# Seven experts in the order of their row counts, with tails of 64, 32 and 0 rows, and a new table of the attention's order

## The chip, the cores and the metric

The kernel runs on one core of one Trainium2 chip. The metric is the device time of one execution in microseconds. Before the change it is 722.44 us, the median of three runs (721.05 to 723.35).

## The reference

An RWKV-7 attention over 4 batches, 8 heads, 768 steps and a head width of 40 gives 3072 tokens of 320 numbers. Each token then goes through one of eight experts, whose sizes are set by the data:

```python
state_decay = state * w_t - outer(state @ a_t, b_t)      # per head, step by step
state = state_decay + outer(v_t, k_t)                    # y_t = r_t @ state, taken before the update
...
logits = x @ w_gate                                      # x: 3072 x 320, 8 experts
expert = argmax(logits);  gate = softmax(logits)[expert]
y[rows of e] = relu(x[rows of e] @ w1[e]) @ w2[e]        # w1: 320 x 1024, w2: 1024 x 320
out = gate * y
```

No row is dropped, so a kernel with fixed block sizes needs a way for the rows that do not fit.

## The kernel before, in words

**Attention.** The 768 steps are cut into 12 chunks of 64, and a chunk is done for two batches at a time: 24 units (`unit(u)`, from L574 on). A unit is some 19 groups of small matmuls on PE (TensorE), with copies, masks, scans and decays between them on ACT, DVE and POOL (ScalarE, VectorE, GpSimd). Names used below: `scan_r`, `scan_q` are scans on DVE; `decay_kb`, `decay_a`, `s2`, `gt_mask`, `st` and `tt_add` (L749) are elementwise work on POOL; `p_last` is the last group of the inverse, `kept` its three copies out of PSUM (two for one half, one for the other), `tt_add` adds to what they left, and `p_q` (operands `TT,O`) is the group that reads it; `t_v` transposes V, `t_u` and `t_st` transpose U and the state, `p_x` (operand `turn_gate`) turns the result and computes the logits.

**The order.** All of this, and the routing and expert 0 with it, is written as `Step` objects with an engine, a cost in us and what they read and write. `in_order` simulates the engines with those costs and issues the steps in the order of that simulation. For units 2 to 22 the order on PE, ACT, DVE and POOL is taken from the table `CYCLE`: for each named step an engine and a key, and `unit + key` is its rank. For steps on SP (loads and stores, SyncE's queue) the key is only a tie-break. PE executes in the order in which it was issued: where the simulated data come earlier than the real ones, PE waits.

**Routing.** After units, `route` works on the logits of one or two chunks: it picks each token's expert (`choose`), counts tokens ahead of it with matmuls, turns the count into a slot (`place`, L1010 to 1035) and adds the token's number to a table `tab` at that slot by a matmul of one-hot rows and columns. Five passes run on POOL, the last two on DVE. The table has 28 columns of 128 slots: for each pair of experts three columns of the first, three of the second, and a column with 64 tail rows of each. `rows_at` turns table entries into gather and scatter indices with 12 small DVE operations. After the last but one pass the counts are raised to at least 384 (L1015), and `g_idx` and `s_idx` are computed for all main columns; after the last pass only the four tail columns are (`gh_idx`, `sh_idx`). So every expert's first 384 rows are known before the last chunk is, and a tail holds the rest, up to 448 rows in all (`CAP`).

**Expert 0** is part of the planned block: its three gathers from `x_rows`, the three of expert 1 and the tail of both share two buffers (`qini`, L1112), each gathered block is turned by three transposes (L1122), and expert 0's 384 rows go through layer 1 and layer 2. Expert 1's weights are loaded into room that the attention frees (`wx`), by SP, while the last units run.

**Experts 1 to 7** follow in a loop (L1274 on). Layer 1 (`layer1`, from L1207 on) multiplies by 448 columns of rows: for each pair of 128 hidden units four whole matmuls (L1217) and two half-height ones (L1225). Every fp32 matmul appears as two in the records. Layer 2 (`layer2`, from L1235 on) has three blocks of 128 rows, each 8 matmuls of 320 columns; after the second expert of a pair comes a block with the tails of both, 64 and 64 rows, at the two halves of the array. Each block is copied by ACT (L1247) and scattered by POOL (L252). In the meantime the next expert's blocks are turned (`turn`, L1203), the next pair's seven blocks gathered (L1195), and the next expert's weights, 2.62 MB in eight transfers, fetched on ACT's queue (L240 to L246). Three rooms for weights are used in turn.

**Overflow.** Rows past 448 are gathered in blocks of 128 by a loop at the end under `tc.If(nx > 0)`; the number of these blocks, `nx`, is counted from the expert counts (L1169 to 1187).

The lines on which the experts' times hang (layer 1 from L1214, its half-height part L1222, and layer 2 from L1238):

```python
for db in range(DB - 1):                                    # L1217: whole matmuls, c1 - c0 columns of rows
    nc.tensor.matmul(hps[i][:, : c1 - c0], lhsT=w[0][:, db, (fb + i) * 128 : (fb + i + 1) * 128], rhs=xT[:, db, c0:c1], ...)
...
hf = slice(i * 64, (i + 1) * 64)                            # L1225: the last 64 of 320, at one half of the array's rows
nc.tensor.matmul(hps[i][:, : c1 - c0], lhsT=w[1][hf, fb // 2, :], rhs=xT[hf, DB - 1, c0:c1], ...)
...
for fb in range(FB):
    r0 = 0
    for w, h, c0, n in parts:                               # L1241: n rows of one expert; a pair's tails are two parts
        nc.tensor.matmul(zp[r0 : r0 + n], lhsT=h[:, fb, c0 : c0 + n], rhs=w[2][:, fb, :], ...)
        r0 += n
```

## Time and profile before

| | |
|---|---|
| median of three runs | 722.44 us |
| profiled execution, its own time | 722.41 us |
| its span | 720.7 us |
| mean granted TensorE clock | 0.98 |
| TensorE matmul busy | 657.8 us, 91% |
| GpSimd, VectorE, ScalarE busy | 402.6, 395.0, 281.4 us |
| DMA | 60.85 MB, mean 84 GB/s |

The profile is one execution. "PE" is matmuls, "PEld" weight loads, a name with a small q (SPq, ACTq) an engine's DMA queue. A line number is that of the kernel; many of the attention's matmuls share the helper L563, so they are told apart by operands. In a row of the timeline the first number is the start, the second the time from the first start to the last end of a run of like instructions, and the bracket is the idle time before it with what ended it. Matmuls are pipelined: the distance from start to start is what one costs in a row of many, not its own duration.

### The profile page before, as it was taken

The page shows a single profiled execution, that of the slowest core. Times are in us where ns is not written, and L with a number is a line of the kernel's source. Part 1 is how long each engine was busy: PE and PEld are TensorE (multiplying, and loading weights), DVE is VectorE, ACT ScalarE, POOL GpSimd, SP SyncE. Part 2 cuts the span into 40 slices and gives each one's busy share as a digit, 9 for nine tenths or more (in the row PEclk, how much of TensorE's full clock was granted, in tenths as well). Part 3 has the DMA queues.
Part 4 walks back from the last instruction along what each step waited for, and adds up shares of the span by engine and source line. Part 5 has one row for each costly group of instructions (what it writes and reads, how often), then busy time and mean ns, then how long its engine had stood idle before and what let it go on. Part 6 is the DMA issues. An engine that isn't in the chain of part 4 may idle for free.

```text
span 720.7 us, 32168 instructions
## 1 busy us (share of the span) xinstructions
PE 657.8 (91%) x13992; PEld 507.0 (70%) x13992; DVE 395.0 (55%) x864; ACT 281.4 (39%) x734; POOL 402.6 (56%) x599
## 2 busy tenths in 40 slices
PE   3679999989989999999889986999999999999995
PEld 2578889878888888889788875556655656464653
DVE  6578988878888988788887785302020101111010
ACT  3356656646556656566556642211011111101110
POOL 8877768897889789778986753132214014110101
PEclk9689999999999999999999999999999999999998
DMA  4432323233333323233322033228343244012000
GB/s 94 98 70 63 85 70 73 70 95 101 73 75 82 82 71 87 71 92 77 86 59 62 25 100 116 67 95 264 119 169 97 82 159 157 25 32 74 25 10 20
DMA packets 120355, 60.85 MB, mean 84 GB/s; under 512 B 100688, under 2 KB 116051, under 8 KB 120212
## 3 DMA queue, kind: packets, MB, share of 16 engines
q1 hardware_dynamic: 103176, 33.09, 18.6%
q10 hardware_dynamic: 13900, 16.23, 7.1%
q0 software_dynamic: 3136, 9.44, 4.0%
q8 instruction: 111, 1.82, 1.1%
q14 instruction: 32, 0.26, 0.1%
HBM read 50.08 MB, written 9.31 MB: 82 GB/s over the span
## 4 chain that ended last, share of the span: by engine, by line
PE 48%; issue 34%; POOL 9%; DMA 4%; DVE 2%; SPq 2%; ACT 1%; POOLq 0%; DVEq 0%; ACTq 0%
PE ps L563 39%; PE ps L667 6%; POOL out_dram L252 4%; PE ps L780 3%; POOL xg L1195 3%; SPq L598 2%; DMA qini<-x_rows,g_idx 1%; DMA KB<-in_packed_dram 1%; POOL KB L627 1%; DMA R<-in_packed_dram 1%; POOL TT L749 1%; DMA Vu<-in_packed_dram 0%; DMA out_dram<-q,s_idx 0%; DMA dec<-in_packed_dram 0%; DVE wx L690 0%
## 5 line engine op out<-in xcount | busy, mean ns | idle before, releaser
L1230 DVE TENSOR_SCALAR h_sb<-hp 128x448 f32<-128x448 f32 (+1 forms) x32 | 18.4, 575 | 191.0 <-PE hp L1225 164.6
L563 PE MATMUL ps<-wx 64*64 64x128 f32 (+1 forms) x3072 | 104.4, 267 | 7.3 <-issue 2.5
L690 DVE TENSOR_TENSOR wx<-ps,wx 64x256 f32<-64x256 f32 (+1 forms) x216 | 90.1, 417 | 26.3 <-PE ps L563 22.2
L677 POOL TENSOR_TENSOR wx<-T,ihalf 64x256 f32<-64x256 f32 x96 | 70.6, 736 | 47.7 <-DVE T L673 34.2
L252 POOL DMA_INDIRECT out_dram<-zo,s_idx x21 | 20.8, 992 | 134.8 <-ACT zo L1247 133.6
L563 PEld LDWEIGHTS ps<-wx 64*64 64x64 f32 x3072 | 81.8, 136 | 20.0 <-issue 11.2
L627 POOL TENSOR_TENSOR KB<-KB,rv 128x512 f32<-128x512 f32 x48 | 71.5, 1493 | 3.0 <-DMA R<-in_packed_dram 1.7
L1241 PE MATMUL zp<-w,h_sb 128*128 128x320 f32 (+1 forms) x272 | 71.0, 433 | 0.0
L1241 PEld LDWEIGHTS zp<-w,h_sb 128*128 128x128 f32 (+1 forms) x272 | 44.4, 174 | 20.5 <-issue 1.3
L723 DVE STREAM_TRANSPOSE wx<-ps 128x512 f32<-128x512 f32 x72 | 51.0, 708 | 12.3 <-PE ps L563 10.4
L552 ACT COPY wx<-ps 128x256 f32<-128x256 f32 (+2 forms) x102 | 43.9, 430 | 33.5 <-PE ps L563 25.9
L1231 ACT ACTIVATE h_sb<-hp 128x448 f32<-128x448 f32 (+1 forms) x32 | 16.1, 505 | 101.0 <-PE hp L1225 50.8
L1241 PE MATMUL zp<-wx,h_sb 128*128 128x320 f32 (+1 forms) x192 | 53.0, 433 | 0.0
L1247 ACT COPY zo<-zp 128x320 f32<-128x320 f32 x25 | 10.7, 427 | 106.0 <-PE zp L1241 96.0
L1217 PE MATMUL hp<-xgT,w 128*128 128x448 f32 x128 | 51.1, 547 | 0.0
L749 POOL TENSOR_TENSOR TT<-TT,wx 128x512 f32<-128x512 f32 x24 | 44.1, 1837 | 11.3 <-DVE pm__173 L965 5.8
L552 ACT COPY ZU<-ps 64x320 f32<-64x320 f32 x92 | 38.7, 421 | 14.4 <-PE ps L667 12.9
L615 DVE TENSOR_TENSOR_SCAN rv<-dec,ones 128x521 f32<-128x521 f32 x24 | 39.3, 1637 | 7.6 <-DMA dec<-in_packed_dram 6.0
L1241 PEld LDWEIGHTS zp<-wx,h_sb 128*128 128x128 f32 (+1 forms) x192 | 33.4, 177 | 13.2 <-issue 0.8
L1217 PEld LDWEIGHTS hp<-xgT,w 128*128 128x128 f32 x128 | 23.5, 190 | 25.8 <-issue 25.5
L667 PE MATMUL ps<-ident,Vu 128*128 128x128 f32 x184 | 30.0, 287 | 11.6 <-DVE rv L615 7.7
L563 PE MATMUL ps<-ZU,nKB 128*64 128x104 f32 (+1 forms) x768 | 39.0, 253 | 1.4 <-issue 1.0
(243 smaller groups left out, 1378.1 us busy)
## 6 DMA issues: line engine op xcount, KB each, us to landing
KB<-in_packed_dram SPq DMA_DIRECT2D x188, 40.0 KB
w<-in_moe_w_dram ACTq DMA_DIRECT2D x16, 320.0 KB
x_rows<-xs SPq DMA_DIRECT2D x24, 192.0 KB
w<-in_moe_w_dram ACTq DMA_DIRECT2D x8, 512.0 KB
dec<-in_packed_dram SPq DMA_DIRECT2D x96, 40.0 KB
Vu<-in_packed_dram SPq DMA_DIRECT2D x96, 40.0 KB
A<-in_packed_dram SPq DMA_DIRECT2D x92, 40.0 KB
R<-in_packed_dram SPq DMA_DIRECT2D x92, 40.0 KB
```

The costliest lines, as they stand in the source:

```text
L252: ins_ = nc.gpsimd.indirect_dma_start(out=out[:, :], out_offset=bass.IndirectOffsetOnAxis(ap=si, axis=0), in_=zo, in_offset=None, bounds_c ...
L552: nc.scalar.copy(dst, src)
L563: nc.tensor.matmul(out_, lhsT=lhsT, rhs=rhs, start=start, stop=stop, skip_group_check=True)
L615: Step(turn_of("scan_r", pre + 0.1), DVE, 1.5, lambda e: nc.vector.tensor_tensor_scan(rv[:, : SEG * C1 + 1][:, ::-1], dec[:, ::-1], ones65 ...
L627: Step(turn_of("decay_kb", pre), POOL, 1.24, lambda e, kb=kb, by=by: nc.gpsimd.tensor_tensor(kb, kb, by, op=ALU.mult), reads=hrv + hKB[2:] ...
L667: nc.tensor.transpose(psum[:, ps.at, p * 128 : (p + 1) * 128], t[:, p].rearrange("x a j -> x (a j)"), ident[:])
L677: Step(turn_of("s2", rk + 0.5), POOL, 0.85, lambda e, z=z, par=par, q=q, X=X: nc.gpsimd.tensor_tensor(X[halves[par], q, :, 2, :], T1[halve ...
L690: nc.vector.tensor_tensor(dst[o_, q], src[o_, q], old[o, q], op=ALU.add)
L723: Step(turn_of(f"x0{k}", rk - 0.4), DVE, 0.72, lambda e, ps=ps, Xn=Xn: nc.vector.transpose(Xn[:, :, :, 0, :], half_sums(ps, 2)[:, :, :, 0, ...
L749: Step(turn_of("tt_add", rk - 1.5), POOL, 1.45, lambda e, X=X, TT=TT: nc.gpsimd.tensor_tensor(TT[:], TT[:], X[:, :, :, 2, :], op=ALU.add), ...
L1217: nc.tensor.matmul(hps[i][:, : c1 - c0], lhsT=w[0][:, db, (fb + i) * 128 : (fb + i + 1) * 128], rhs=xT[:, db, c0:c1], start=(db == 0 and n ...
L1241: nc.tensor.matmul(zp[r0 : r0 + n], lhsT=h[:, fb, c0 : c0 + n], rhs=w[2][:, fb, :], start=(fb == 0), stop=(fb == FB - 1), skip_group_check ...
```

## The change

Expert 0 stays as it was, with a tail of 64 rows. The other seven are no longer run as 1 to 7 but by place: on the chip they are sorted by their final counts, the largest at place 1. The tail of a place is fixed: 64 rows at places 0 and 1, 32 at places 2 to 5, none at 6 and 7. A place's layer 1 has 384 columns and its tail; a pair's tail block has twice the tail rows, and the pair of places 6 and 7 has no tail block, gather or transpose of one. The table has four columns for each expert, 32 in all. Expert 0's three columns are turned into indices after the last but one pass. For the seven others the table is permuted by place and turned into indices after the last pass, so place 1's gathers and weights come after that too. Weights of places are fetched by SP, at an address that SP reads from the sorted list into a register. Behind the block a few small DVE operations work out each expert's cap for the overflow count.

The table `CYCLE` is new as a whole, and eight costs of steps are other numbers: `scan_r` 1.66 for 1.5, `scan_q` 1.45 for 1.6, `decay_kb` 1.57 for 1.24, `decay_a` 1.36 for 1.24, `tt_add` 1.95 for 1.45, `st` 0.8 for 0.85, `x0` 0.73 for 0.72 and `xs_pad` 0.3 for 0.2. In the order of units 2 to 22 that it gives, `kept` is on ACT with all three copies (one was on DVE), both `x14` copies on ACT (one was on DVE), one of the two `nkb` copies on DVE, `tt_add` follows `gt_mask` on POOL with a `decay_kb` behind it (which stood between them before), `t_st` and `t_u` change places on PE, and `t_v` runs one unit earlier, ahead of `p_x`.

The diff, cut to its core:

```diff
+    PJ = NJ + 1
+    TAIL = (64, 64, 32, 32, 32, 32, 0, 0)
-    NS = E // 2 * PB
+    NS = E * PJ
...
+    def by_count():
+        v = nc.vector
+        v.scalar_tensor_tensor(key[:], in0=ptr[:, 1:], scalar=16.0, in1=iota_f[:, : E - 1], op0=ALU.mult, op1=ALU.subtract)
+        v.tensor_tensor(
+            over[:], key[:, None, :].to_broadcast([128, E - 1, E - 1]), key[:].unsqueeze(2).to_broadcast([128, E - 1, E - 1]), op=ALU.is_gt,
+        )
+        v.tensor_reduce(place_of[:], over[:], axis=AX, op=ALU.add)
+        v.tensor_tensor(
+            perm[:], place_of[:, None, :].to_broadcast([128, E - 1, E - 1]),
+            iota_f[:, : E - 1].unsqueeze(2).to_broadcast([128, E - 1, E - 1]), op=ALU.is_equal,
+        )
+        v.tensor_tensor(order_f[:], perm[0:1], iota_f[0:1, None, 1:E].to_broadcast([1, E - 1, E - 1]), op=ALU.mult)
+        v.tensor_reduce(order_s[:], order_f[:], axis=AX, op=ALU.add)
+        v.tensor_copy(order_i[:], order_s[:])
+
+    def in_places():
+        v = nc.vector
+        perm_tab = sc[:].rearrange("x i b e -> x (i b e)")[:, : (E - 1) * PJ * (E - 1)].rearrange("x (p j e) -> x p j e", p=E - 1, j=PJ)
+        v.tensor_tensor(
+            perm_tab, perm[:].unsqueeze(2).to_broadcast([128, E - 1, PJ, E - 1]),
+            tab[:, PJ:].rearrange("x (e j) -> x j e", j=PJ)[:, None].to_broadcast([128, E - 1, PJ, E - 1]), op=ALU.mult,
+        )
+        to = tab_o[:].rearrange("x (e j) -> x e j", j=PJ)
+        v.tensor_reduce(to, perm_tab, axis=AX, op=ALU.add)
+        v.tensor_copy(to[64:, 0, NJ : NJ + 1], to[:64, 0, NJ : NJ + 1])
+        v.tensor_copy(to[:64, 0, NJ : NJ + 1], tab[:64, NJ : NJ + 1])
+        for i in (1, 3):
+            v.tensor_copy(to[32:64, i, NJ : NJ + 1], to[:32, i + 1, NJ : NJ + 1])
...
+    def expert_at(p):
+        ex = nc.sync.value_load(order_i[0:1, p - 1 : p], min_val=0, max_val=E - 1)
+        return moe_w1[bass.ds(ex, 1)].rearrange("o d f -> (o d) f"), moe_w2[bass.ds(ex, 1)].rearrange("o f d -> (o f) d")
...
-        "decay_a": [(POOL, -3.864)], "decay_kb": [(POOL, -4.773), (POOL, -5.136)], "exp": [(ACT, 0.625)], "first": [(ACT, -0.339)], "gk": [(ACT, -1.196)],
-        "gt": [(ACT, -1.911), (ACT, -2.054)], "gt_mask": [(POOL, -3.227)], "kept": [(ACT, -0.804), (DVE, -0.900)],
-        "minus": [(ACT, -0.232)], "n1": [(DVE, -2.300), (DVE, -2.340)], "nkb": [(ACT, -2.768), (ACT, -2.661)], "off": [(ACT, -2.089), (ACT, -1.875)],
-        "p_y": [(PE, -0.237)], "p_z": [(PE, -0.500)], "pc": [(ACT, -2.625)], "q": [(ACT, -0.482)], "recip": [(DVE, -3.140)], "rhs": [(ACT, -0.696)],
-        "t_kb": [(PE, -3.132)], "t_st": [(PE, -0.395)], "t_u": [(PE, -0.447)], "t_v": [(PE, -1.921)], "tt_add": [(POOL, -2.045)],
-        "xs_pad": [(POOL, -0.409)], "xt": [(DVE, 0.060)], "zu": [(DVE, -0.180), (DVE, -0.220)],
+        "decay_a": [(POOL, -3.864)], "decay_kb": [(POOL, -4.955), (POOL, -5.591)], "exp": [(ACT, 0.183)], "first": [(ACT, -0.883)], "gk": [(ACT, -1.717)],
+        "gt": [(ACT, -2.317), (ACT, -2.483)], "gt_mask": [(POOL, -3.136)], "kept": [(ACT, -1.250), (ACT, -1.283)],
+        "minus": [(ACT, -0.750)], "n1": [(DVE, -2.196), (DVE, -2.239)], "nkb": [(DVE, -2.587), (ACT, -3.150)], "off": [(ACT, -2.417), (ACT, -2.350)],
+        "p_y": [(PE, -0.342)], "p_z": [(PE, -0.605)], "pc": [(ACT, -3.117)], "q": [(ACT, -0.950)], "recip": [(DVE, -3.804)], "rhs": [(ACT, -1.217)],
+        "t_kb": [(PE, -3.237)], "t_st": [(PE, -0.553)], "t_u": [(PE, -0.500)], "t_v": [(PE, -3.079)], "tt_add": [(POOL, -2.045)],
+        "xs_pad": [(POOL, 0.318)], "xt": [(DVE, 0.152)], "zu": [(DVE, -0.109), (DVE, -0.065)],
...
-            Step(turn_of("scan_r", pre + 0.1), DVE, 1.5, lambda e: nc.vector.tensor_tensor_scan(
+            Step(turn_of("scan_r", pre + 0.1), DVE, 1.66, lambda e: nc.vector.tensor_tensor_scan(
-            Step(turn_of("scan_q", pre - 1.0), DVE, 1.6, lambda e: nc.vector.tensor_tensor_scan(
+            Step(turn_of("scan_q", pre - 1.0), DVE, 1.45, lambda e: nc.vector.tensor_tensor_scan(
-                Step(turn_of("decay_kb", pre), POOL, 1.24, lambda e, kb=kb, by=by: nc.gpsimd.tensor_tensor(kb, kb, by, op=ALU.mult),
+                Step(turn_of("decay_kb", pre), POOL, 1.57, lambda e, kb=kb, by=by: nc.gpsimd.tensor_tensor(kb, kb, by, op=ALU.mult),
-            Step(turn_of("tt_add", rk - 1.5), POOL, 1.45, lambda e, X=X, TT=TT: nc.gpsimd.tensor_tensor(TT[:], TT[:], X[:, :, :, 2, :], op=ALU.add), reads=hX[3:], writes=hTT)
+            Step(turn_of("tt_add", rk - 1.5), POOL, 1.95, lambda e, X=X, TT=TT: nc.gpsimd.tensor_tensor(TT[:], TT[:], X[:, :, :, 2, :], op=ALU.add), reads=hX[3:], writes=hTT)
...
-                    v.tensor_scalar(ptr[:], ptr[:], scalar1=float(MAIN), scalar2=None, op0=ALU.max)
+                    v.tensor_scalar(ptr[:, :1], ptr[:, :1], scalar1=float(MAIN), scalar2=None, op0=ALU.max)
...
-                for i in range(2):
-                    v.tensor_tensor(pm[:, :, 1 + i], sl_c, offs[:, None, i].to_broadcast([128, n, E]), op=ALU.mult)
+                v.tensor_tensor(pm[:, :, 1], sl_c, offs[:, None].to_broadcast([128, n, E]), op=ALU.mult)
                 folded(v, pm)
-                r, off, half = (pm[:, :, i, 0] for i in range(3))
+                r, off = (pm[:, :, i, 0] for i in range(2))
                 v.tensor_copy(rank_c, r)
-                v.tensor_scalar(sl, r, scalar1=MAIN - 0.5, scalar2=None, op0=ALU.is_ge)
-                v.tensor_tensor(sl, sl, half, op=ALU.mult)
-                v.tensor_tensor(so, r, off, op=ALU.add)
-                v.tensor_tensor(sl, sl, so, op=ALU.add)
+                v.tensor_tensor(sl, r, off, op=ALU.add)
...
             if c1 + 1 == NCH:
-                Step(rk, DVE, 2.2, lambda e: rows_at(nc.vector, tab[:], [t[:] for t in tmp], g_idx[:], s_idx[:]), reads=[h_tab], writes=[h_idx[0], h_itmp])
+                Step(rk, DVE, 2.4, lambda e: rows_at(nc.vector, tab[:, :NJ], [t[:, :NJ] for t in tmp], g0_idx[:], s0_idx[:]), reads=[h_tab], writes=[h_idx[0], h_itmp])
             if c1 == NCH:
-                halves_ = tab[:, PB - 1 :: PB]
-                Step(rk, DVE, 2.2, lambda e: rows_at(
-                    nc.vector, halves_, [t[:, : E // 2] for t in tmp], gh_idx[:], sh_idx[:],
-                ), reads=[h_tab], writes=[h_idx[1], h_itmp])
+                Step(rk, DVE, 1.3, lambda e: by_count(), reads=[h_ptr], writes=[h_order])
+                Step(rk, DVE, 1.2, lambda e: in_places(), reads=[h_tab, h_order], writes=[h_tab_o, h_tmp])
+                Step(rk, DVE, 2.6, lambda e: rows_at(
+                    nc.vector, tab_o[:], [t[:, : (E - 1) * PJ] for t in tmp], g_idx[:], s_idx[:],
+                ), reads=[h_tab_o], writes=[h_idx[1], h_itmp])
 
...
+        def first_expert(e):
+            parts.clear()
+            fetch(weights[1], *expert_at(1), lambda part, *_: parts.append(part))
+        places = []
+        fetch(weights[1], moe_w1[1], moe_w2[1], lambda part, *where: places.append(where))
+        Step(NU, SP, 1.5, first_expert, reads=[h_order], writes=[h_w1], lag=0.2)
+        for i, (lo, hi) in enumerate(places):
             under = [h for _, held in r_X.bufs[(at_ + lo) // XN : (at_ + hi - 1) // XN + 1] for h in held]
-            Step(NU, SP, 0.4, lambda e, part=part: part(), writes=[h_w1] + under, lag=4)
+            Step(NU, SP, 0.4, lambda e, i=i: parts[i](), writes=[h_w1] + under, lag=4)
...
+                first = j < NJ
                 nc.gpsimd.indirect_dma_start(
-                    out=xg, out_offset=None, in_=x_d[: N if half else EARLY, :],
-                    in_offset=bass.IndirectOffsetOnAxis(ap=gh_idx[:, 0:1] if half else g_idx[:, j : j + 1], axis=0),
+                    out=xg, out_offset=None, in_=x_d[: EARLY if first else N, :],
+                    in_offset=bass.IndirectOffsetOnAxis(ap=g0_idx[:, j : j + 1] if first else g_idx[:, j - NJ : j - NJ + 1], axis=0),
-            Step(rk, POOL, 1.25, rows_in, reads=[h_idx[half]], writes=hxg, after=stores if half else stores[: NU - BH], lag=2.5)
+            Step(rk, POOL, 1.25, rows_in, reads=[h_idx[j >= NJ]], writes=hxg, after=stores if j >= NJ else stores[: NU - BH], lag=2.5)
...
+    cap_e = rte.tile([128, E], F32)
+    nc.vector.memset(cap_e[:, :1], float(CAP))
+    steep = rte.tile([128, E - 1], F32)
+    nc.vector.tensor_scalar(cap_e[:, 1:], place_of[:], scalar1=0.5, scalar2=float(TAIL[1] - TAIL[2]), op0=ALU.is_le, op1=ALU.mult)
+    nc.vector.tensor_scalar(steep[:], place_of[:], scalar1=4.5, scalar2=float(TAIL[2]), op0=ALU.is_le, op1=ALU.mult)
+    nc.vector.scalar_tensor_tensor(cap_e[:, 1:], in0=cap_e[:, 1:], scalar=float(MAIN), in1=steep[:], op0=ALU.add, op1=ALU.add)
+    past = rte.tile([128, E], F32)
+    nc.vector.tensor_sub(past[:], ptr[:], cap_e[:])
...
+        blocks = [(i * NJ + j, col(2 * k + i, j)) for i in range(2) for j in range(NJ)]
+        if TAIL[2 * k]:
+            blocks.insert(NJ, (PB - 1, col(2 * k, NJ)))
...
+        if i == 0 and TAIL[p]:
+            turn(xgs[k][2 * NJ], *((xTs[p + a], TAIL[p] * a, TAIL[p], MAIN) for a in range(2)))
...
+            weights[p + 1] = wx_room if (p + 1) % 3 == 1 else room(w_pool if (p + 1) % 3 else w_first)
+            fetch(weights[p + 1], *expert_at(p + 1), lambda part, *where: parts.append(part))
+        layer1(w, xTs[p], h, 0, MAIN + TAIL[p], parts[: FB // 2])
...
-            layer2(sh_idx[:, k : k + 1], *((weights[x], hs[x], MAIN, 64) for x in (e - 1, e)))
+            if TAIL[p]:
+                layer2(rows_to(max(p - 1, 1), NJ), *((weights[x], hs[x], MAIN, TAIL[x]) for x in (p - 1, p)))
```

More of the change, by code (lines that the diff above doesn't have):

```diff
@@ L1288 @@
             parts = []
-        if e + 1 < E:
-            turns(e + 1)
+        if p + 1 < E:
+            turns(p + 1)
         if i == 0 and k + 1 < E // 2:
```

119 lines of the change are left out of this document (64 added, 55 removed).

## The prediction

> **What bounds the kernel now.** I read the page's slices first, then busy time by stage, then TensorE's waits, then the timeline of each stage that the diff touches. Stage rows give busy us and count for each engine, then the granted clock, the DMA share and GB/s.
>
> ```profile
> span 720.7 us, 32168 instructions
> PE   3679999989989999999889986999999999999995
> PEclk9689999999999999999999999999999999999998
> ```
>
> ```profile
> 60.00:415.00 355.00, 333.66 (x11292) 301.00 (x11290) 295.76 (x606) 212.40 (x570) 288.40 (x433) 1.00 0.31 75
> 415.00:449.87 34.87, 25.80 (x868) 22.59 (x865) 24.25 (x99) 13.19 (x37) 14.30 (x21) 0.99 0.35 106
> 449.87:479.27 29.40, 28.77 (x109) 18.02 (x108) 6.16 (x39) 5.85 (x15) 4.26 (x6) 0.96 0.18 59
> 479.27:712.50 233.23, 233.22 (x911) 134.61 (x911) 29.47 (x56) 26.39 (x56) 44.71 (x46) 1.00 0.31 101
> ```
>
> Four stages are to be seen: attention in steady state, its last units with the routing, expert 0, and the seven experts. In the last TensorE is busy 233.22 of 233.23 us, so a matmul taken out there shortens the kernel by its own time. In attention TensorE idles 355 - 333.66 = 21.3 us, and most of that is no wait for data:
>
> ```profile
> PE ps L563 <- issue: 15.6, 31, 2.1
> ```
>
> This leaves 21.3 - 15.6 = 5.7 us in which another engine or a DMA was late.
>
> **The experts' matmuls.** The end of the kernel (start, us, engine):
>
> ```profile
> 665.20 0.82 PE L1203 MATMUL tp<-ident,xg 128*128 128x128 f32 x6
> ...
> 683.92 6.28 PE L1217 MATMUL hp<-xgT,wx 128*128 128x448 f32 x16
> 690.13 1.77 PE L1225 MATMUL hp<-xgT,wx 64*128 64x448 f32 x8
> 691.84 3.27 PE L1217 MATMUL hp<-xgT,wx 128*128 128x448 f32 x8
> 694.95 13.08 PE L1241 MATMUL zp<-wx,h_sb 128*128 128x320 f32 x48
> 707.96 0.48 PE L1241 MATMUL zp<-w,h_sb 128*64 128x320 f32 x1
> ...
> 712.05 0.43 PE L1241 MATMUL zp<-wx,h_sb 128*64 128x320 f32 x1
> ```
>
> Sixteen 448-column matmuls start in 6.28 us, the last taking 0.55: a step of (6.28 - 0.55)/15 = 0.382 us. Of 320 columns it is (13.08 - 0.43)/47 = 0.269. So a column costs (0.382 - 0.269)/128 = 0.00088 us. Layer 1 of an expert has 32 such steps, and 16 half-height matmuls that run in pairs (8 take 1.77, four steps): 40 steps. Places 2 to 5 lose 32 columns: 40 x 32 x 0.00088 = 1.13 us each, 4.5 in all. Places 6 and 7 lose 64: 2.25 each, 4.5. By plain proportion (0.382 x 32/448 for 32 columns) the sum is 8.7 rather than 9.0; I take 8.8.
>
> The tail of the last pair goes: the last matmul ended at 712.05 + 0.43 = 712.48 and would end at 694.95 + 13.08 = 708.03, 4.45 us sooner. Nothing covers that, and the output copy and scatter behind it only move up. Place 6 turns no tail block: three transposes at (0.82 - 0.28)/5 = 0.11, 0.33 us. The tails of 32 rows in layer 2 save nothing:
>
> ```profile
> L1241 PE MATMUL zp<-w,h_sb 128*128 128x320 f32 x192 | 53.0, 432 | 0.0
> ...
> L1241 PE MATMUL zp<-w,h_sb 128*64 128x320 f32 x80 | 18.1, 435 | 0.0
> ```
>
> Half the stationary columns take as long, 435 against 432 ns. Sum here: 8.8 + 4.45 + 0.33 = 13.6 us.
>
> **Place 1 becomes known late.** Its rows and weights now wait for the final counts. What stands there:
>
> ```profile
> 449.20 0.88 PE L1122 MATMUL ps<-ident,qini 128*128 128x128 f32 x3 [0.72 <-DMA qini<-x_rows,g_idx]
> ...
> 477.07 1.24 PE L563 MATMUL ps<-w,nKB 128*128 128x320 f32 x4
> ...
> 479.27 3.27 PE L1217 MATMUL hp<-wx 128*128 128x448 f32 x8 [0.63 <-ACT wx L552]
> ```
>
> ```profile
> 449.45 0.32 DVE L1171 TENSOR_TENSOR og<-ptr,thr 128x168 f32<-128x168 f32 x1
> 449.80 0.33 DVE L1175 TENSOR_REDUCE ovt<-og 128x8 f32<-128x168 f32 x1
> ...
> 456.03 0.18 DVE L1053 TENSOR_TENSOR tab<-tab,ps 128x28 f32<-128x28 f32 x1 [2.27 <-PE ps L563]
> ...
> 457.05 0.17 DVE L201 CAST gh_idx<-idx_tmp 128x4 int32<-128x4 f32 x1
> ```
>
> ```profile
> qini<-x_rows,g_idx POOLq DMA_INDIRECT x6, 3.4
> ```
>
> ```profile
> DMA packets 3245, 5.49 MB, mean 249 GB/s; under 512 B 317, under 2 KB 2365, under 8 KB 3244
> xg<-x_rows,g_idx POOLq DMA_INDIRECT x6, 5.7
> ```
>
> The last two fences are DMA views of 430 to 452 us and of 478 to 500, when weights were loading; the last number is us from issue to landing. A gain first: the transposes at 449.20 belong to expert 1 and stood ahead of expert 0's first matmul, waiting 0.72 us for their rows. Those rows are now gathered later: -0.7.
>
> The chain: the table is whole at 456.2. `by_count` (7 small operations at 0.2 apart) fits the 2.27 us in which VectorE waited there. `in_places` takes two operations like L1171 and L1175 (0.65) and four at 0.2: 1.5. The cast of the gather index comes 1.0 after the table, as before (457.05). Up to seven more small operations of the capacity count behind the block can slip in, 1.4. The first gather thus starts at 458.7 to 460.1, the second 1.3 later. Two buffers serve four gathers, so the third waits until the first is turned (1 us). With landings of 3.4 to 5.7 the rows stand ready at 469 to 475; expert 0's layer 2 keeps TensorE until 478.3. So they are covered, by 3 to 9 us. TensorE is in order, though, and its place for each transpose was planned: a landing later than planned stops it, at most 5.7 - 3.4 = 2.3 us in each of two rounds. Bounds 0 and 4.6; the plan allows 1.25 + 2.5 = 3.75, near the 3.4 row: +1.0.
>
> By the Trainium skill (DMA: Bandwidth & Descriptors, Anatomy of one DMA) a DMA takes about 2.0 us plus its bytes over 436 GB/s. For 128 rows of 1536 bytes that estimate is 2.45, the stop would be 0, and the sum 1 us lower; the trace disagrees, with 3.4 and 5.7 us.
>
> SP's queue takes place 1's weights:
>
> ```profile
> 450.45 0.38 SPq L246 DMA_DIRECT2D wx<-in_moe_w_dram  x1
> ```
>
> The last of them was issued at 450.45; now the first cannot go before about 455. Their 2.62 MB at 249 GB/s take 10.5 us, so they land near 468, ten before layer 1 asks. Behind the register read that waits on SP are only these DMAs, since the last x stores are ready earlier. Later fetches move from ACT's queue to SP's. Each has a place's 30 us for 10.5 us of transfer: 0, and nothing on TensorE waited for ACT's issues. No row shows a DMA addressed by a register; with SP otherwise idle I take 0 to 1.5 us an expert, all covered.
>
> **Routing.** Four small operations leave each pass. In the last passes they are VectorE's, and one lay on the chain that ended last:
>
> ```profile
> 428.32 1.25 DVE L1022 TENSOR_SCALAR sl__174<-pm__173 128x2 f32<-128x2 f32 x1
> ```
>
> Bounds: 0, and 1.25 + 3 x 0.2 = 1.9; its neighbour probably inherits most of the stall: -0.5.
>
> **The attention order.** TensorE's order keeps its cycle, but for t_u against t_st and t_v, which runs one unit earlier, just ahead of p_x. A cycle of before:
>
> ```profile
> 204.96 1.55 SPq L598 DMA_DIRECT2D Vu<-in_packed_dram  x4
> ```
>
> ```profile
> 210.37 0.69 PE L563 MATMUL ps<-wx 64*64 64x64 f32 x32
> ...
> 214.17 1.12 PE L563 MATMUL ps<-turn_gate,xT 128*128 128x88 f32 x8
> ...
> 215.67 0.69 PE L563 MATMUL ps<-TT,O 64*64 64x64 f32 x32
> ```
>
> ```profile
> 212.26 2.12 POOL L627 TENSOR_TENSOR KB<-KB,rv 128x512 f32<-128x512 f32 x1
> 214.34 1.28 POOL L749 TENSOR_TENSOR TT<-TT,wx 128x512 f32<-128x512 f32 x1
> ...
> 218.34 1.18 POOL L627 TENSOR_TENSOR KB<-KB,rv 128x512 f32<-128x512 f32 x1
> ```
>
> ```profile
> 211.19 0.75 ACT L552 COPY TT<-ps 64x256 f32<-64x256 f32 x2 [2.13 <-PE ps L563]
> ```
>
> ```profile
> 345.27 2.59 DMA R<-in_packed_dram
> ```
>
> The V load that t_v will need is issued by 206.5 and, landing like R in 2.6, is there at 209.1; t_v comes at about 214.2. Covered by 5 us.
>
> In this unit, which carries routing on POOL, p_q starts at 215.67 on the heels of tt_add (214.34 + 1.28 = 215.62), which had stood behind decay_kb (L627) although its ACT copies were done at 211.94. The new POOL order puts tt_add ahead of decay_kb, up to 2 us sooner. Against that, the third copy of `kept` goes from VectorE to ACT, 0.38 us (0.75/2) later on that chain. Bounds: all 21.3 us of idle gained; or 0.38 lost in each of the 22 units between the first and the last, 8.4. Nearest is the 5.7 us of real waits, of which I take half: -2.8.
>
> **Sum.** -13.6 - 0.7 + 1.0 - 0.5 - 2.8 = -16.6. The profiled execution took 722.41 us (span 720.7), the median is 722.44: 705.8.
>
> **Rivals.**
>
> *The order gains more.* If issue waits shrink as well and half the idle goes (10.7 rather than 2.8), the time is 698. For: 15.6 us are there. Against: the instructions, and nearly their order, are the same.
>
> *Place 1 is not covered.* If its transposes are planned ahead of expert 0's layer 2, TensorE idles from about 464.5 to 475: 10 us, and the time is 715. For: all its inputs now hang on the last table. Against: the 3 to 9 us of cover. The stage from 449.87 already ran at clock 0.96. The Trainium skill (TensorE: Matmul & The Clock Gate, Part 1) says that an idle window of 3.4 us halves the clock until 3.4 us of work are done. That is 1.7 us more here, so 717 by the page; the row fits it, with 0.04 x 29.4 = 1.2 us lost.
>
> *`kept` costs its 0.38 us in every unit:* +8.4 instead of -2.8, 717. Against: ACT idled 2.13 us just before those copies.
>
> *Slower: POOL in its long form.* The same decay_kb took 1.18 us at 218.34 and 2.12 at 212.26. If the new order meets VectorE so that five more POOL operations of a routing unit run long, that unit loses 5 x 0.94 = 4.7 us, having no slack at p_q; five routing passes make 23.5, and 729. It decides from 13.8/5 = 2.8 us a unit on. For: 215.62 against 215.67. Against: four POOL operations leave each pass.
>
> *The places do not hold.* A count above its place's cap opens the overflow loop: 2.62 MB of weights (10.5 us), 40 steps of 128 columns (4.5), 16 of 320 (4.3) and a gather (3.4) that nothing covers, behind a second set of one-hot tables: 22.7 us and more, above 728. Against: the reference's own routing counts 423, 414, 388, 375, 371, 357, 323 rows for the sorted seven, under 448, 416 four times and 384 twice.
>
> **Chances.** Forecast 0.66 (702 to 711); more gain 0.12; place 1 uncovered 0.10; `kept` 0.04; POOL 0.06; overflow 0.02. The range goes from 696.5 (the first rival with no stop at place 1 and 1 us of routing) to 717, and leaves out 0.08 above. A measurement of this kernel tells about 0.3% (2.2 us) from no change: faster 0.90, same 0.02, slower 0.08.
>
> **What would show it.** L1217 at 416 columns 27 ns a step quicker, at 384 twice that; no pair tail after the last 128-row block; from place 1's layer 1 to the last matmul 219.6 us rather than 233.2; that layer 1 starting within 2 us of expert 0's end; TensorE idle of 16 to 21 us in the steady units. Wrong would be an idle TensorE inside the experts, p_q starting over 0.6 us later after p_last than the 5.3 us here, or an overflow block.

## The result, and the profile after

The changed kernel takes 701.08 us (median of 6 runs, 696.38 to 705.29), the kernel before, run beside it, 720.64 (717.24 to 723.35). The ratio is 0.972 with a 95% interval of 0.969 to 0.976: faster by 2.8%. Here and below, medians are of the runs within 1.5% of their kernel's fastest; two of e3's eleven and two of e5b's four lay beyond. The profiled execution took 702.67 us, with a span of 700.9 us against 720.7.

The head of the page of the changed kernel, in the same 40 slices as before:

```profile
span 700.9 us, 32091 instructions
PE   2688999999999999999998987989999999999995
PEclk9889999999999999999999999999999999999998
```

The same stages, each row with busy us and count for PE, PEld, DVE, ACT and POOL, then the granted clock, the DMA share and GB/s:

```profile
60.00:415.00 355.00, 337.72 (x11485) 304.93 (x11486) 294.03 (x590) 216.99 (x594) 280.36 (x424) 1.00 0.31 76
415.00:440.95 25.95, 18.70 (x651) 15.91 (x648) 16.32 (x68) 9.09 (x26) 4.88 (x6) 1.00 0.16 49
440.95:474.18 33.23, 30.57 (x114) 19.18 (x114) 11.10 (x67) 7.54 (x21) 6.28 (x8) 0.95 0.37 119
474.18:692.94 218.76, 218.75 (x876) 130.55 (x876) 27.48 (x54) 25.07 (x55) 42.65 (x44) 1.00 0.35 107
```

Expert 0 starts at 440.95 instead of 449.87, 8.9 us sooner. Expert 0 itself, up to place 1's layer 1, takes 33.23 us instead of 29.40, which gives 3.8 back. The seven experts take 218.75 instead of 233.22, and TensorE is still never idle in them: 14.5 less. Together that is 19.6 of the 19.8 us by which the span is shorter. TensorE's idle time from 60 to 415 us went from 21.3 to 355 - 337.72 = 17.3 us.

The matmuls of places 2 and 6 and the last block:

```profile
518.62 5.85 PE L1273 MATMUL hp<-xgT,w 128*128 128x416 f32 x16
...
642.71 5.43 PE L1273 MATMUL hp<-xgT,w 128*128 128x384 f32 x16
...
679.85 13.08 PE L1297 MATMUL zp<-wx,h_sb 128*128 128x320 f32 x48
```

Sixteen steps of layer 1 took 6.28 us with 448 columns; they take 5.85 with 416 (27 ns a step less) and 5.43 with 384 (53 ns less). Nothing follows the last 128-row block.

What became longer is the place where place 1's rows enter:

```profile
457.39 0.70 PE L606 MATMUL ps<-w,Vu 128*128 128x320 f32 x2
460.13 0.52 PE L1170 MATMUL ps<-ident,qini 128*128 128x128 f32 x3 [2.03 <-DMA qini<-x_rows,g_idx]
...
462.05 0.85 PE L1170 MATMUL ps<-ident,qini 128*128 128x128 f32 x3
```

```profile
453.98 0.97 POOL L1160 DMA_INDIRECT qini<-x_rows,g_idx  x1 [11.07 <-DVE idx_tmp L247]
455.26 0.95 POOL L1160 DMA_INDIRECT qini<-x_rows,g_idx  x1 [0.30 <-PE ps L606]
460.92 0.95 POOL L1160 DMA_INDIRECT qini<-x_rows,g_idx  x1 [4.71 <-PE ps L1170]
```

TensorE stands for 2.03 us in front of the first transposes, until 460.13, for a gather that GpSimd issued at 453.98: 6.1 us from issue to use. Then three transposes take 0.85 us at 462.05 where they take 0.49 at 466.27.

### The profile page after: what moved, and what is told of

The parts are those of the page before. It is cut to its first block, busy times and chain, and to the rows that moved or that the text cites. A ratio compares the mean times of both kernels' runs of the same rounds, so it can differ in the third digit from the quotient of the medians.

```text
span 700.9 us, 32091 instructions
## 1 busy us (share of the span) xinstructions
PE 644.0 (92%) x13957; PEld 503.5 (72%) x13957; DVE 389.1 (56%) x850; ACT 283.7 (40%) x755; POOL 386.6 (55%) x575
## 5 line engine op out<-in xcount | busy, mean ns | idle before, releaser
L1286 DVE TENSOR_SCALAR h_sb<-hp 128x416 f32<-128x416 f32 (+3 forms) x32 | 17.3, 542 | 190.2 <-PE hp L1281 161.0
L1297 PE MATMUL zp<-w,h_sb 128*128 128x320 f32 (+2 forms) x256 | 66.4, 433 | 0.0
L670 POOL TENSOR_TENSOR KB<-KB,rv 128x512 f32<-128x512 f32 x48 | 58.6, 1224 | 5.5 <-DMA Vu<-in_packed_dram 2.1
L1297 PEld LDWEIGHTS zp<-w,h_sb 128*128 128x128 f32 (+2 forms) x256 | 41.4, 172 | 18.7 <-issue 3.0
L1287 ACT ACTIVATE h_sb<-hp 128x416 f32<-128x416 f32 (+3 forms) x32 | 15.3, 477 | 92.7 <-PE hp L1281 44.0
L1297 PE MATMUL zp<-wx,h_sb 128*128 128x320 f32 (+2 forms) x176 | 48.5, 433 | 0.0
L1273 PE MATMUL hp<-xgT,w 128*128 128x416 f32 (+1 forms) x128 | 46.8, 514 | 0.0
L700 POOL TENSOR_TENSOR GT<-GT,m_low 128x512 f32<-128x512 f32 x24 | 33.3, 1388 | 16.0 <-DVE wx L766 11.7
L1297 PEld LDWEIGHTS zp<-wx,h_sb 128*128 128x128 f32 (+2 forms) x176 | 30.8, 178 | 13.4 <-issue 2.6
L1251 POOL DMA_INDIRECT xg<-x_rows,g_idx x20 | 19.2, 961 | 37.7 <-PE tp L1259 30.0
```

The lines of the kernel that those rows point to most:

```text
L670: Step(turn_of("decay_kb", pre), POOL, 1.57, lambda e, kb=kb, by=by: nc.gpsimd.tensor_tensor(kb, kb, by, op=ALU.mult), reads=hrv + hKB[2:] ...
L700: Step(turn_of("gt_mask", rk), POOL, 1.33, lambda e, d=dst_, m=mask: nc.gpsimd.tensor_tensor(d, d, m, op=ALU.mult), writes=held)
L1251: nc.gpsimd.indirect_dma_start(out=xg, out_offset=None, in_=x_d[:, :], in_offset=bass.IndirectOffsetOnAxis(ap=gi, axis=0),)
```

## The experiments

Three questions: is the gain the sum of its parts, why does expert 0 take longer, and which part of the new order pays? Twelve kernels. "Attention" is the time from the first t_kb in the steady units to expert 0's first matmul, "expert 0" from there to place 1's layer 1, "experts" from there to the last matmul; all three in the one profiled execution.

```
kernel                        median  ratio (95%)               attention expert 0 experts
before                        720.4   1                         378.0     29.4     233.2
after                         701.1   0.9723 (0.9685-0.9762)    369.1     33.2     218.8
e1  order alone               713.6   0.9901 (0.9870-0.9932)    369.2     29.3     233.2
e2  places, old order         705.9   0.9794 (0.9764-0.9825)    373.0     31.5     218.8
e3  all tails 64              713.7   0.9920 (0.9886-0.9954)    366.3     34.1     232.3
e9  tails 64,64,32,32,0...    691.6   0.9618 (0.9578-0.9657)    362.9     33.4     211.5
e10 rows planned later        694.5   0.9639 (0.9601-0.9677)    363.9     31.0     218.8
e11 e10 with e9's tails       686.7   0.9542 (0.9503-0.9580)    366.8     29.3     211.5
e5  chain late, not planned   698.8   0.9724 (0.9681-0.9767)    362.3     36.1     218.8
e5b chain late, planned       694.4   two: 691.06, 697.69       366.8     30.9     218.8
e7  t_v back                  697.4   0.9701 (0.9662-0.9741)    366.1     31.6     218.8
e8  t_v only                  718.6   0.9981 (0.9957-1.0005)    372.4     29.8     233.2
e13 GpSimd's order back       703.8   0.9775 (0.9735-0.9816)    375.0     33.4     218.8
e6  ascending                 757.3   one run                   370.1     33.2     218.8 + loop
```

The kernel before ran beside each group with a median of 718.5 to 720.4, so ratios are compared, not times of different groups.

### Do the parts add up?

**Order alone** (e1): the new CYCLE table and the planner's costs of the attention steps in the kernel before. (Eleven costs differ, not eight: besides those named ahead, `gt_mask` is 1.33 for 1.3, `t1` 0.74 for 0.73 and `s2` 0.74 for 0.85.)

> The kernel before with only the new attention order: the CYCLE table and the planner's costs of the attention steps are the changed kernel's, while experts, places and routing stay as before. Theory (the parts add up, and the attention gain comes from the table): the nineteen steady units, from the first t_kb to the last, shrink by 4.7 us as they did in the changed kernel (326.8 to 322.1), nothing else moves, and the ratio to the kernel before is 716.0/720.6 = 0.9935. Rival (the attention gain belongs to the shorter routing passes, and the table is worth nothing): no change, 1.000, and VectorE and GpSimd still meet as often, with tt_add near 1.84 us. My own prediction had 2.8 us for the order, a ratio of 0.996.

**Places, old order** (e2): the reverse, the old table and costs in the changed kernel.

> The changed kernel with the old CYCLE table and the old costs of the attention steps; places, tails and routing stay as changed. Theory (additive): the 4.7 us of the steady units are lost again and the rest is kept, 701.1 + 4.7 = 705.8, a ratio of 0.979. Rival (shorter routing passes give the attention gain): the steady units stay near 322 us, and the ratio is 0.973, that of the changed kernel.

By its ratio e1 gained 7.1 us (interval 4.9 to 9.4), and by theirs e2 is 5.1 behind the changed kernel; 0.9901 x 0.9794 = 0.970, beside 0.972 measured. The parts add up, the rival of e1 (1.000) is out, and the order is worth about 5 to 7 us, more than I gave it. The place was not as expected, though. Of the 8.8 us of attention that e1's profiled execution saves, only 1.8 lie in the nineteen steady units (326.8 to 325.0), the rest in the last units before expert 0. And e2, with the old order, takes 323.5 us for the steady units, nearer to the 322 of its rival than to 326.8. In which units the order pays is not shown.

**All tails 64** (e3):

```diff
-    TAIL = (64, 64, 32, 32, 32, 32, 0, 0)
+    TAIL = (64,) * 8
...
-        for i in (1, 3):
-            v.tensor_copy(to[32:64, i, NJ : NJ + 1], to[:32, i + 1, NJ : NJ + 1])
+        for i in (1, 3, 5):
+            v.tensor_copy(to[64:, i, NJ : NJ + 1], to[:64, i + 1, NJ : NJ + 1])
```

(and the capacity's threshold from place 4 to place 6)

> The changed kernel with tails of 64 rows at all seven places: sorting, places and the new order stay, but no column and no tail block is saved. Theory (the places pay only through the sizes that they allow, and finding the order on the chip is covered): the experts take back 8.5 us of layer-1 columns, 4.45 us of the last pair's tail and 0.33 us of a transpose, 13.3 in all, so 714.4 and a ratio of 0.991. Rival (sorting itself pays or costs, through the later start of the first gather or weights on another queue): more than 3 us away from 714.4; if the sort chain costs what the two gains of the start hide, 717 or more.

713.7 us and 0.992, where 714.4 and 0.991 were expected: the tails that the sorting allows are worth about 14 us (0.992 less 0.972). What sorting itself costs is seen in expert 0, 34.1 us here against 29.4 before. The experts of e3:

```profile
471.49:703.77 232.28, 232.27 (x911) 133.98 (x911) 29.46 (x56) 26.31 (x56) 44.62 (x46) 1.00 0.33 102
```

By this stage the tails are worth 232.27 - 218.75 = 13.5 us. The 0.95 us between 233.22 and 232.27 are no tails. They are in place 1, where expert 0's 64 tail rows go through layer 1. Before, then after:

```profile
495.20 1.00 PE L1217 MATMUL hp<-xT,w 128*128 128x64 f32 x8
496.13 0.66 PE L1225 MATMUL hp<-xT,w1c 64*128 64x64 f32 x6
496.72 0.66 PE L1217 MATMUL hp<-xT,w 128*128 128x64 f32 x4
497.31 0.43 PE L1225 MATMUL hp<-xT,w1c 64*128 64x64 f32 x2
...
501.80 0.43 PE L1241 MATMUL zp<-wx,h_sb 128*128 128x320 f32 x1
```

```profile
490.12 1.00 PE L1273 MATMUL hp<-xT,w 128*128 128x64 f32 x8
491.05 0.66 PE L1281 MATMUL hp<-xT,w1c 64*128 64x64 f32 x8
491.64 2.00 PE L1273 MATMUL hp<-xT,w 128*128 128x64 f32 x16
...
495.76 0.70 PE L1297 MATMUL zp<-wx,h_sb 128*128 128x320 f32 x2
```

The same 48 matmuls alternate between the full array and its halves (128\*128 and 64\*128 in the rows) in groups of 8, 6, 4 and 2 before, and of 8 and 16 after. With the same six transposes among or behind them they take 6.60 us against 5.64. The function that issues them is the same in both; the order in which they came out is not, and why is not shown.

**Shorter tails** (e9), a version that the counts allow: `TAIL = (64, 64, 32, 32, 0, 0, 0, 0)`, copies for `i in (1,)`, the threshold from place 4 to place 2.

> The changed kernel with tails 64, 64, 32, 32 and then none for the last four places; the sorted counts 375, 371, 357 and 323 of these four all fit 384 rows. Theory: places 4 and 5 lose 32 columns each (1.06 us each, as places 2 and 3 lost 15.93 - 14.87), the tail block of their pair goes (4.45 us) and one transposed block (0.33 us): 6.9 us less than the changed kernel, 694.2, a ratio of 0.963. Rival (the tail block in the middle hides something, the output copy or the next pair's rows, that then stops TensorE): less than half of that, 698 and a ratio of 0.968 or more.

691.6 us and 0.962: faster than the changed kernel, with the experts at 211.53 us, 7.2 less (6.9 expected).

### Why expert 0 takes longer

Theory: place 1's rows are covered, but the transposes stand too early in TensorE's fixed order. **Rows planned later** (e10):

```diff
-            Step(rk, POOL, 1.25, rows_in, ..., lag=2.5)
+            Step(rk, POOL, 1.25, rows_in, ..., lag=5.0 if j >= NJ else 2.5)
```

> The changed kernel, in which the planner is told that a gather of place 1 lands 5.0 us after its issue instead of 2.5. Nothing is computed differently: TensorE's fixed order only puts place 1's four transposed blocks further back among expert 0's layer-2 matmuls. Theory (place 1's chain costs about 4 us although its rows are covered, because the first transposes stand too early in TensorE's order: it stopped 2.03 us for them and ran 1.8 us behind at a lower pace after the stop): the stretch from expert 0's first matmul to place 1's layer 1, 33.2 us in the changed kernel against 29.4 before, falls to 29.7, and the time to 697.5, a ratio of 0.968. Rival (the stretch is long for another reason, such as the weights of place 1 or the gathers themselves): it stays above 32.5, and the time is 700 to 702.

**With the shorter tails** (e11), both edits in one kernel.

> Both edits together: the later plan for place 1's rows, and tails of 64, 64, 32, 32 and none for the last four places. Theory (they are in different stages and add up): 691.6 - 3.5 = 688.1, a ratio of 0.956. Rival (the plan is worth nothing): 691 to 692, the time of the tails alone, a ratio of 0.962.

Two kernels delay the chain by twenty small VectorE copies ahead of `in_places`. **Chain late, not planned** (e5):

```diff
     def in_places():
         v = nc.vector
+        for _ in range(20):
+            v.tensor_copy(sc[:, 1], sc[:, 0])
```

> The changed kernel with twenty small idle copies on VectorE (about 0.2 us each, 4 us in all) ahead of the step that brings the table into the order of the places; the planner isn't told, so TensorE's order stays. Theory (TensorE stops for the rows where its order has the transposes, whatever other work is ready): the stop of 2.03 us grows to about 6, the stretch from expert 0's first matmul to place 1's layer 1 from 33.2 to 37, and the time to 705, a ratio of 0.978. Rival (the 3 to 9 us of cover that my prediction counted hide the delay): the stretch stays within 1 us of 33.2 and the time at 701 to 702.

**Chain late, planned** (e5b): the same, and the step's cost for the planner is 7.2 us instead of 1.2.

> The same twenty copies, with the planner told that the step takes 6 us more. Theory (cover is there, but only an order that knows of the delay can use it): TensorE takes the transposes later, the stop goes, and the stretch is 29.5 to 31 us although the chain is 4 us longer; the time is 697 to 700, quicker than the changed kernel without the copies. Rival (delay costs in either order, since the last rows now come after expert 0's layer 2): the stretch is 34 us or more, and the time over 702.

The stretch of expert 0 in e10, cut in two, in e11, in e5 and in e5b:

```profile
435.45:445.00 9.55, 9.54 (x27) 5.93 (x28) 6.54 (x43) 1.11 (x5) 0.24 (x1) 0.82 0.06 21
445.00:466.46 21.46, 20.83 (x89) 13.31 (x87) 4.57 (x25) 6.44 (x16) 6.09 (x7) 1.00 0.57 175
```

```profile
437.71:467.03 29.32, 28.69 (x114) 18.26 (x114) 11.03 (x66) 7.54 (x21) 6.32 (x8) 1.00 0.42 135
```

```profile
433.58:469.69 36.11, 31.85 (x114) 20.01 (x114) 14.89 (x87) 7.54 (x21) 6.26 (x8) 0.91 0.34 110
```

```profile
438.30:469.20 30.90, 29.07 (x114) 18.19 (x114) 14.89 (x87) 7.62 (x21) 7.17 (x8) 1.00 0.42 133
```

With the later plan the stop is gone in e10 and e11, and where the clock stays at 1.00 the stretch is 29.3 us, as before the change. In e10 it is 31.0, with a clock of 0.82 in the first 9.55 us. The twenty copies took 4.53 us. With the chain so much later the stretch is 36.1 us when the order is the old one and 30.9 when the planner knows: the cover that I had counted is there, and only an order that knows the true landing can use it. For e5 and e5b this rests on the stretch; the times (698.8, and 691.06 and 697.69) do not settle it, since attention, which the copies do not touch, differed by 4.5 us between the two profiled executions.

The stop in e5 grew to 3.63 us and not to the 6 that I expected:

```profile
454.35 0.87 PE L1172 MATMUL ps<-ident,qini 128*128 128x128 f32 x3 [3.63 <-DMA qini<-x_rows,g_idx]
```

```profile
451.06 0.97 POOL L1162 DMA_INDIRECT qini<-x_rows,g_idx  x1 [15.53 <-DVE idx_tmp L249]
```

```profile
GB/s 0 0 18 146 300 337 364 437 391 324 272 327 240 274 333 330 370 370 370 367 249 26 0 61 154 215 109 205 130 0 0 0 0 82 208 147 0 0 0 77
```

The last row is e5's DMA traffic from 442 to 460 us, in slices of 0.45 us. The copies hold up the gather, but not place 1's weights, which were through at about 452. The gather, issued at 451.06 as they ended, took 3.3 us from issue to use, where it took 6.1 in the changed kernel.

How much of the changed kernel's 3.8 us is the clock is seen in these rows, the changed kernel after its stop and then e7 (below), whose stop of 2.04 us is the same:

```profile
460.13:466.27 6.14, 6.14 (x20) 4.30 (x21) 0.00 (x0) 1.39 (x3) 2.91 (x3) 0.72 0.23 67
```

```profile
456.90:461.35 4.45, 4.45 (x20) 3.25 (x21) 0.00 (x0) 1.38 (x3) 2.89 (x3) 1.00 0.28 80
```

The same matmuls take 6.14 us at a granted clock of 0.72 and 4.45 at 1.00, 1.7 us between them, and so are the whole stretches (33.23 and 31.55). In the changed kernel the stop cost its 2.03 us, and 1.7 of pace were lost behind it. In the Trainium skill (TensorE: Matmul & The Clock Gate, Part 1) a clock falls after an idle window of 3.4 us; here stops of 2.03 us (the changed kernel) and 2.20 (e9) were followed by a lower clock, 0.62 and 0.65 over the next 4 us, and stops of 2.04 (e7) and 2.65 (e3) by 1.00, so the trace does not bear the 3.4 us out as a bound below which a stop is free. What decides between the two outcomes is not shown.

### Which part of the order pays

**t_v back** (e7): t_v's key -2.026 and its copies' -2.0 and -1.9, so that it runs behind p_x in its own unit again.

> The changed kernel with one entry of the new attention order taken back: t_v (and the copies that follow it) runs where it ran before, in the unit that it belongs to and behind p_x, rather than one unit earlier and ahead of p_x. All else is new. Theory (the order pays through TensorE's order: fewer of its stops are 'issue' waits, which were 14.5 and 13.4 us between 72 and 388 us in the two kernels with the old table and 8.3 to 12.2 in the seven with the new): issue waits are 13 us or more again, the time is 4 to 5 us up, 705.5, a ratio of 0.979. Rival (the gain lies in the other engines' orders, or in TensorE's nowhere): issue waits of 8 to 12 and a ratio of 0.972.

**t_v only** (e8): the early t_v and its copies in the kernel before.

> The kernel before with that one entry alone: t_v one unit earlier and ahead of p_x, its copies earlier too; costs, other orders, experts and routing as before. Theory (TensorE's order pays): issue waits of 8 to 12 us between 72 and 388 us instead of 14.5, and a ratio of 0.994. Rival (the other engines' orders pay): 1.000 within the interval, issue waits of 13 to 15.

**GpSimd's order back** (e13): in the changed kernel the keys of all steps on GpSimd are the old ones, for example:

```diff
-        "decay_kb": [(POOL, -4.955), (POOL, -5.591)],
+        "decay_kb": [(POOL, -4.773), (POOL, -5.136)],
```

> The changed kernel with GpSimd's operations in their old order (tt_add behind decay_kb again), all else new. My prediction gave the order its 2.8 us for just this: tt_add ahead of decay_kb. By it the waits of TensorE for GpSimd come back (TT 1.0 us between 72 and 388 us before, none in the changed kernel), VectorE and GpSimd meet more often (decay_kb near 1.49 us rather than 1.22), and the time is 2.8 us up, a ratio of 0.976. Rival (GpSimd's order is off the path, and the gain lies in TensorE's own order or in VectorE's and ScalarE's): 0.972, with decay_kb and tt_add as long as before and no wait on them.

My theory for e7 and e8 fell: taking t_v back costs nothing (0.970 beside 0.972), and t_v alone gives nothing that the interval tells from 1. GpSimd's order does pay: e13 is at 0.9775 where e7, on the same chip, is at 0.970, 5 to 6 us apart, and the changed kernel is at 0.972, 4 apart, though its interval overlaps with e13's. Attention points the same way over all the kernels: with GpSimd's old order (before, e2, e8, e13) it takes 372.4 to 378.0 us, with the new one in ten kernels 362.3 to 370.1, without overlap. But the first three of the four have old orders on other engines too, and e13's profiled execution took 709.79 us where its median is 703.8. Two of GpSimd's groups from 72 to 388 us, before, after and in e13, and for the last two also `st` (behind the first bar stand the busy us and the mean in ns, behind the second GpSimd's idle time before them and what ended it):

```profile
L627 POOL TENSOR_TENSOR KB<-KB,rv 128x512 f32<-128x512 f32 x38 | 59.0, 1554 | 0.0
L749 POOL TENSOR_TENSOR TT<-TT,wx 128x512 f32<-128x512 f32 x19 | 37.7, 1984 | 5.6 <-DVE sa L891 5.0 <-ACT TT L552 0.4
```

```profile
L670 POOL TENSOR_TENSOR KB<-KB,rv 128x512 f32<-128x512 f32 x37 | 43.8, 1184 | 1.5 <-DVE rv L658 1.2
L792 POOL TENSOR_TENSOR TT<-TT,wx 128x512 f32<-128x512 f32 x19 | 27.7, 1456 | 12.8 <-ACT TT L595 12.0 <-DMA KB<-in_packed_dram 0.7
...
L839 POOL TENSOR_TENSOR ST<-sa,pc 128x320 f32<-128x320 f32 x19 | 23.2, 1223 | 0.0
```

```profile
L719 POOL TENSOR_TENSOR KB<-KB,rv 128x512 f32<-128x512 f32 x38 | 69.5, 1829 | 1.2 <-DVE rv L707 1.2
L841 POOL TENSOR_TENSOR TT<-TT,wx 128x512 f32<-128x512 f32 x19 | 25.5, 1340 | 1.5 <-ACT TT L644 1.5
...
L888 POOL TENSOR_TENSOR ST<-sa,pc 128x320 f32<-128x320 f32 x19 | 13.7, 723 | 0.0
```

(The line numbers of e13 are shifted, its table being written out longer.) In the new order GpSimd reaches tt_add before ScalarE's copies are done and waits for them, 12.0 us in all; before, it came to it later and waited 0.4. decay_kb ran in its short form nearly always, 1.18 us, and with the old order so often in its long one that the means are 1.55 and 1.83. In e13 its 38 runs cost GpSimd 24 us more than after. But `st`, which got longer in the new order, takes 9.5 less there, so that GpSimd is busy for 259.0 us instead of 251.7 in this window, and the kernel lost some 4 to 6 us. How GpSimd's order reaches TensorE is not shown: the waits of TensorE for tt_add, 1.0 us before and none after, are 0.3 in e13, where 1.0 was expected.

### The price of an overflow

**Ascending** (e6): `is_gt` becomes `is_lt` where `by_count` compares the keys, so that two counts pass their places' caps.

> The changed kernel sorting the other way (smallest count first), so that the two largest experts, 414 and 423 rows, stand at the places for 384: two blocks overflow. It prices my last rival, which gave at least 22.7 us for the first block (weights 10.5, 40 + 16 matmul steps 8.8, a gather 3.4) behind a second set of tables. Theory (nothing covers the loop): 2 x 22.7 and 5 to 15 us of tables, 750 to 765 us. Rival (the loop loads the second block's weights beside the first, and the tables beside the last place): 725 to 745.

```profile
693.51 0.75 PE L1406 MATMUL zp<-xo_c,xo_r 128*128 128x24 f16 x24
702.44 0.88 PE L1259 MATMUL tp<-ident,xg 128*128 128x128 f32 x3 [8.18 <-DMA xg<-x_rows,gi]
...
734.11 0.88 PE L1259 MATMUL tp<-ident,xg 128*128 128x128 f32 x3 [15.29 <-DMA xg<-x_rows,gi]
```

757.3 us in one run, inside the range of the theory: 56 us for two blocks, 28 each. The tables were built beside the last place, and the first block's weights loaded early; the second waited 15.29 us for rows, and between 702.44 and 734.11 lie 31.7 us for one block.

## Why the prediction was right, and which steps were not

The forecast was 705.8 us in 696.5 to 717, the result 701.1. The total held partly because two misses had opposite signs.

**The experts' matmuls, -13.6.** Right: 13.5 by e3 and the changed kernel. The experts took 14.5 off in all; the rest is place 1's 64-column matmuls, which alternate less often, and no step of mine looked at their order.

**Place 1's transposes, +1.0, bounds 0 to 4.6.** The size failed. The stretch became 3.8 us longer: 2.03 of stop, 1.7 of clock, and one more block that is turned inside it. The step that failed is the value between the bounds: "the plan allows 1.25 + 2.5 = 3.75, near the 3.4 row". The landing took 6.1 us, longer than both rows that I had (3.4 and 5.7). The DMA view of 452 to 470 us shows what ran beside it:

```profile
DMA  9998999999999999710000057100853360000000
GB/s 419 419 428 311 298 273 232 250 313 378 364 378 370 378 384 406 262 38 0 0 0 0 0 92 280 65 0 0 143 222 108 137 216 11 0 0 0 0 0 0
```

Up to about 460 us the DMA engines are full with place 1's weights, at 232 to 428 GB/s. Weights and rows hang on the same chain: the weights were issued from 449.65 to 454.80, the first gather at 453.98. I costed both, the weights at 10.5 us "ten before layer 1 asks", and never the one against the other. The 3.4 row was no guide, since it came from 430 to 452 us of the kernel before, where the DMA engines moved 118 GB/s in the mean. e5 takes the two apart: issued as the weights ended, the gather took 3.3 us. The first gather came 3.4 us after the table (453.98 against 450.62), within the 2.5 to 3.9 forecast.

**The cover of 3 to 9 us.** Right as a cover, as e5b showed, wrong as a protection: TensorE stops at a fixed place. The rival "place 1 is not covered" (715 to 717) did not come true, but its mechanism did at a third of its size, clock included.

**The start of expert 0, -0.7.** Not to be found by itself: TensorE now stops 0.60 and 0.72 us for expert 0's own rows instead. And the 1.2 us that I put down to the clock of 0.96 there were hardly any: e1 ran this stretch at 1.00 in 29.27 us, against 29.40.

**Routing, -0.5.** Too small to be separated. e2 was 14.5 us faster than the kernel before; the experts gave 14.5 and expert 0 took back 2.1, so some 2 us are left for routing and all else before expert 0.

**Attention order, -2.8.** Mis-sized: 5 to 7 us by e1 and e2. That GpSimd's order pays was right, by e13. That it pays by letting p_q start sooner, as I argued, is not shown: from p_last to p_q it is 5.39 us in the mean of the 19 units between 72 and 388 us, before and after alike, and 5.55 in e13, 3.0 us more over all of them, where single units scatter from 5.0 to 6.9. The size came from TensorE's waits of 5.7 us, half of them. Between 72 and 388 us its waits for other engines and DMA fell from 5.1 to 1.8 us, which is near that; but "issue" waits shrank as well. They were:

```profile
PE ps L563 <- issue: 14.5, 29, 2.1
```

```profile
PE ps L606 <- issue: 11.1, 23, 0.9
```

first before, then after; these are the waits at the main helper line. With those at other lines they fell from 14.5 to 12.0; the ten kernels with GpSimd's new order have 8.3 to 12.2 us, the four with the old one 12.0 to 14.5. So the first rival ("issue waits shrink as well", 10.7 us) was true in kind and about half true in size. Why these stops would depend on GpSimd's order stays open.

**The other rivals.** ScalarE's third copy of `kept` cost little: from p_last to p_q it is 5.33 us (median of the same 19 units) against 5.13, inside the 0.6 that I had set. GpSimd's long form became rarer for decay_kb and tt_add, and `st` became longer (0.77 to 1.22 us); GpSimd's busy time fell in all, from 264.1 to 251.7 us between 72 and 388. The places held, and an overflow costs 28 us a block (e6), where I had 22.7 and more.

## What to carry to other kernels

Cover is no property of a chain alone: on an engine that runs in order, work hides a late input only if it stands ahead of the instruction that needs it, so a step that becomes data-dependent needs its landing time in the plan measured anew (here 3.75 us planned from issue to landing, 6.1 taken, 4 us lost, and regained by changing one number). When two transfers hang on one newly late value, cost them against each other. And when sizes are sorted, look at the counts before choosing the steps: tails of 64, 64, 32, 32 and none, with the later plan, take 686.7 us, 0.954 (0.950 to 0.958) of the kernel before, the fastest version here.

## What the runs showed beside

A program of the same instruction order was not the same in every profiled execution: with GpSimd's new order attention took 362.3 to 370.1 us in ten kernels that do the same there (but e1, with the old routing, and e7, with the late t_v), and six runs of the changed kernel spread over 1.3%. The 0.3% that I gave as the resolution of a measurement is too fine; five rounds gave intervals of 0.2 to 0.4% to either side.

TensorE's "issue" waits often follow one another at 3.6 to 4.2 us. Three in the kernel before:

```profile
267.92 0.56 PE L563 MATMUL ps<-rhs,TT 64*64 64x40 f32 x23 [0.41 <-issue]
271.81 0.68 PE L563 MATMUL ps<-R,Vu 64*64 64x64 f32 x28 [0.58 <-issue]
275.64 0.33 PE L563 MATMUL ps<-R,S 64*64 64x64 f32 x4 [0.18 <-issue]
```

They are 3.89 and 3.83 us apart, and from one to the next there are 256 instructions of TensorE, 128 matmuls and 128 weight loads:

```profile
267.92:271.81 3.89, 3.31 (x128) 2.84 (x128) 3.00 (x9) 2.54 (x7) 3.04 (x15) 1.00 0.03 8
271.81:275.64 3.83, 3.65 (x128) 3.28 (x128) 2.83 (x6) 2.91 (x8) 3.09 (x12) 1.00 0.47 106
```

This holds throughout: in each of the 14 kernels all "issue" waits between 72 and 388 us, 18 to 29 of them, lie a multiple of 256 such instructions apart, give or take one. The Trainium skill (Runtime: NRT & Kernel Launch, Instruction fetch mechanics) says that an engine refills its instructions in blocks of 256 while it runs, and that this is mostly hidden. The traces fit such refills showing through at the ends of blocks, 29 of 79 in the kernel before. Why some of these ends cost a stop and others none is not shown.
